# Batch 0 of a Fourier mixing and GELU kernel: part of the second inverse table on VectorE, its copies in another order, fewer spare matmuls at the last table

## The chip, the cores and the metric

One Trainium2 chip, one core of it. The metric is the device time of one execution in microseconds (us), as the median of several runs. Each profile is of one execution, and its own "span" is about 1.8 us shorter than the time measured for that execution.

## The reference

A filter in the frequency domain along the sequence, then a two-layer feed-forward block with exact GELU:

```python
# x: (8, 3008, 256); filt_r, filt_i: (1505, 256); w_in: (256, 2048); w_out: (2048, 256)
X = np.fft.rfft(x, axis=1)
Y = X * (filt_r + 1j * filt_i)[None]
y = np.fft.irfft(Y, n=x.shape[1], axis=1).astype(np.float32).reshape(-1, 256)
h = y @ w_in
g = 0.5 * h * (1.0 + erf(h / sqrt(2)))
return (g @ w_out).astype(np.float32)          # (24064, 256)
```

## The kernel before

The kernel transforms batch 0 as fast as it can (the "front", up to about 40 us), then starts a stream of feed-forward matmuls, into which the transforms of batches 1 to 7 are woven. Only the front is touched. In it, PE is TensorE, DVE is VectorE, ACT is ScalarE and POOL is GpSimd.

The inverse transform needs a table `T3` of 24 slices and a second one, `T3i`, with real and imaginary columns swapped and signed. Both are made from `T2` in three thirds of 8 slices. PE transposes a third into one PSUM bank, and somebody copies it out:

```python
def table_3(self, q):                       # PE, 8 transposes
    self.t3 = ps = self.bank("ps_t3", "n", BF16)
    for i in range(8):
        self.nc.tensor.transpose(ps[:, 128 * i:128 * i + 128], self.T2[:, 8 * q + i]..., self.eye)

def table_3_copy(self, q, turn):            # ACT: T3, and with turn also T3i, from PSUM
    v = self.t3.rearrange("p (k n r) -> p k r n", k=8, r=2)
    self._evac(self.T3[:, 8 * q:8 * q + 8], v, "act")
    if turn:
        for r in range(2):
            self._evac(self.T3i[:, 8 * q:8 * q + 8, r, :], v[:, :, 1 - r, :], "act", self.turn[r])

def table_3_turn(self, q):                  # DVE: T3i from T3 in SBUF (line 256)
    k = slice(8 * q, 8 * q + 8)
    for r in range(2):
        self.nc.vector.tensor_scalar(out=self.T3i[:, k, r, :], in0=self.T3[:, k, 1 - r, :],
                                     scalar1=self.turn[r], scalar2=None, op0=ALU.mult)
```

The work of the front per pair of frequencies (`p` from 0 to 11): `c1t` transposes the data and copies it to `b_sb`, `c2` is two matmuls (line 408) and one DVE product with the filter `F` (line 412), `c3` is the inverse by `T3` and `T3i` (line 430, 16 matmuls for two products). `ps` of `c2` has two PSUM banks, so the matmuls of product p wait for product p - 2.

```python
def c1t(self, q, eng):
    ...                                     # 8 transposes, 4 pairs' worth of data
    n = 1024 // len(eng)
    for i, e in enumerate(eng):             # "act": ScalarE, False: VectorE
        self._evac(b[...][:, n * i:n * i + n], ps[:, n * i:n * i + n], e)

def c2(self, p):
    ...                                     # two matmuls into ps
    nc.vector.tensor_tensor(out=w, in0=ps.unsqueeze(1).to_broadcast([128, 2, 512]),
                            in1=self.F[:, :, 2 * p:2 * p + 2, :]..., op=ALU.mult)
```

Half of `F` is loaded, the other half is a copy. POOL makes these copies for all but the first four frequencies, one instruction (line 97) per product from product 2 on. The loads come in three groups of frequencies (0 to 3, 4 to 11, 12 to 23) in POOL's own DMA queue, behind the loads of x:

```python
for k, n in ((0, 4), (4, 8), (12, 12)):
    m.load_filters(k, n)
m.load_w_in()
nc.gpsimd.memset(m.vt[:, :, 96, :], 0.0)
m.dup_filters(nc.gpsimd, 4, 20)             # POOL, products 2 to 11
...                                         # stage 1 (c1), first third of the table
m.table_3(1)
m.dup_filters(nc.vector, 0, 4)              # DVE, products 0 and 1
m.warm_up(1)                                # spare matmul: nobody reads its result
m.c1t(0, (act, False))
m.table_3_copy(1, True)
m.c1t(1, (act,))
m.c2(0)
m.warm_up(1)
m.c2(1)
m.c1t(2, (act,))
m.warm_up(2)
for q in range(1, 7):
    if q < 6:
        m.c2(2 * q)
        if q + 2 < 6:
            m.c1t(q + 2, (act,))
        m.warm_up(2)
        m.c2(2 * q + 1)
    if q == 3:
        m.table_3(2)
        m.table_3_copy(2, True)
    if q < 6:
        m.c3(2 * q - 2)
        m.warm_up(1)
    ...                                     # the last two inverses
```

## Time and profile before

| | before |
|---|---|
| time, first 6 runs | 773.70 us (773.54 to 773.86) |
| time, all 37 runs of this study | 773.58 us (773.26 to 774.27) |
| span of the trace | 771.8 us |
| first feed-forward matmul (line 482) | 39.94 us |
| from there to the end | 731.9 us |

The table is read from the bottom up. What follows 39.94 us is one PE-bound stream whose length no part of the change touches, so the change is worth what it does to 39.94. The engines, the chain and DVE's products are shown in the prediction.

### The profile page before, as it was taken

Reading aid. Unit: us, or ns where it says so; the run is one execution under the profiler, and the core shown is the slowest. Engines: PE = TensorE matmul, PEld = TensorE weight load, DVE = VectorE, ACT = ScalarE, POOL = GpSimd, SP = SyncE. Lnnn points to the kernel's source line nnn. Section 1 sums busy time; section 2 is a strip of 40 time slices with the busy share of each in tenths; the row PEclk is TensorE's granted clock in tenths of the full one; section 3 lists DMA queues with packets and bytes.
Section 4 is the critical chain, followed back from the end, with each engine's and each line's share of the span. In section 5 each row is a group of like instructions: output and inputs, shape, how many; then the busy total and the mean of one; then the engine's idle time right before and its main releaser. Section 6 shows DMA issues by size and latency. Waiting matters only on the chain.

```text
span 771.8 us, 15050 instructions
## 1 busy us (share of the span) xinstructions
PE 763.7 (99%) x6060; PEld 527.3 (68%) x6060; DVE 397.7 (52%) x734; ACT 568.3 (74%) x980; POOL 63.0 (8%) x154
## 2 busy tenths in 40 slices
PE   7999999999999999999999999999999999999998
PEld 4847675676776766667677767666776776766666
DVE  8856755464545645457463664637646366411011
ACT  7879955897568975699656996579865798666663
POOL 7701100010000200011000110001100000000000
DMA  9894745366253661636516464355553422410111
GB/s 151 147 184 111 153 115 128 128 127 147 58 154 94 137 162 40 193 76 122 143 54 181 85 133 123 81 152 97 122 137 82 138 83 69 123 42 28 42 42 55
DMA packets 87270, 85.66 MB, mean 111 GB/s; under 512 B 6688, under 2 KB 77472, under 8 KB 87200
## 3 DMA queue, kind: packets, MB, share of 16 engines
q1 hardware_dynamic: 78816, 68.70, 31.4%
q0 software_dynamic: 8384, 16.00, 14.8%
q8 instruction: 47, 0.77, 0.4%
q14 instruction: 23, 0.19, 0.1%
HBM read 54.00 MB, written 46.66 MB: 130 GB/s over the span
## 4 chain that ended last, share of the span: by engine, by line
PE 97%; DMA 1%; DVE 1%; POOL 0%; ACT 0%; issue 0%; POOLq 0%; DVEq 0%; SPq 0%
PE ps_o L509 42%; PE ps_h L482 42%; PE ps_s L369 2%; PE ps_s L344 2%; PE ps_s L319 2%; PE ps_s L296 2%; DMA x_sb<-in_x_dram 1%; PE ps_c L430 1%; PE ps_c3t L445 0%; DMA d_sb<-R 0%; PE ps_warm L263 0%; POOL x_sb L83 0%; PE ps_c L408 0%; PE ps_c L459 0%; PE ps_c1t L395 0%; PE ps_e L499 0%
## 5 line engine op out<-in xcount | busy, mean ns | idle before, releaser
L485 ACT ACTIVATE g_sb<-ps_h 128x512 bf16<-128x512 f32 x752 | 438.0, 597 | 183.4 <-PE ps_h L482 172.6
L509 PE MATMUL ps_o<-w_out_sb,g_sb 128*128 128x256 bf16 x2992 | 447.6, 273 | 0.0
L482 PE MATMUL ps_h<-y_sb,w_in_sb 128*128 128x512 bf16 (+3 forms) x1600 | 445.8, 366 | 0.7 <-DVE y_sb L273 0.7
L509 PEld LDWEIGHTS <-g_sb 128*128 128x128 bf16 x2992 | 283.8, 98 | 134.3 <-issue 9.9
L482 PEld LDWEIGHTS <-w_in_sb 128*128 128x128 bf16 x1600 | 154.7, 98 | 23.7 <-issue 1.9
L515 DVE COPY ost<-ps_o 128x512 f32<-128x512 f32 x93 | 63.8, 686 | 143.5 <-PE ps_o L509 143.5
L327 DVE TENSOR_TENSOR p<-ps_s,F 128x512 bf16<-128x512 f32 x84 | 58.1, 691 | 105.9 <-ACT p L326 89.4
L273 DVE TENSOR_SCALAR y_sb<-ps_s 128x376 bf16<-128x376 f32 x112 | 60.9, 548 | 80.8 <-PE ps_s L369 80.8
L271 DVE CAST a_sb<-ps_s 128x512 bf16<-128x512 f32 x112 | 69.3, 682 | 27.7 <-PE ps_s L296 27.7
L271 DVE CAST v_sb<-ps_s 128x512 bf16<-128x512 f32 x84 | 57.4, 684 | 3.0 <-PE ps_s L344 3.0
L325 ACT ACTIVATE p<-ps_s 64x512 bf16<-64x512 f32 x84 | 49.8, 593 | 2.0
L326 ACT CAST p<-ps_s 64x512 bf16<-64x512 f32 x84 | 48.5, 577 | 1.0
L369 PEld LDWEIGHTS <-d_sb 96*128 96x128 bf16 x448 | 30.8, 97 | 25.6 <-DMA d_sb<-R 0.6
L102 POOL COPY gate<-p 1x1 bf16<-1x1 bf16 x48 | 8.5, 176 | 471.5 <-DVE p L329 471.5
L329 DVE TENSOR_TENSOR p<-p 128x512 bf16<-128x512 bf16 x84 | 35.7, 425 | 2.9
L369 PE MATMUL ps_s<-T,d_sb 96*128 96x94 bf16 x448 | 36.3, 204 | 0.1
L328 DVE TENSOR_TENSOR p<-p,F 128x512 bf16<-128x512 bf16 x84 | 34.9, 415 | 0.0
L83 POOL DMA_DIRECT2D x_sb<-in_x_dram x64 | 32.6, 511 | 13.3 <-issue 12.8
L344 PE MATMUL ps_s<-p,T 128*128 128x256 bf16 x168 | 32.1, 273 | 0.0
L319 PE MATMUL ps_s<-b_sb,T 128*128 128x256 bf16 x168 | 32.1, 273 | 0.0
L344 PEld LDWEIGHTS <-T 128*128 128x128 bf16 x168 | 16.4, 98 | 20.0 <-DVE p L329 0.5
L319 PEld LDWEIGHTS <-T 128*128 128x128 bf16 x168 | 16.4, 98 | 13.4
(113 smaller groups left out, 196.6 us busy)
## 6 DMA issues: line engine op xcount, KB each, us to landing
out_dram<-ost SPq DMA_DIRECT2D x93, 256.0 KB, 2.4
x_sb<-in_x_dram POOLq DMA_DIRECT2D x64, 188.0 KB, 3.8
R<-a_sb SPq DMA_DIRECT2D x112, 96.0 KB, 2.1
b_sb<-R SPq DMA_DIRECT2D x28, 384.0 KB, 4.2
R<-v_sb SPq DMA_DIRECT2D x42, 256.0 KB, 3.5
d_sb<-R SPq DMA_DIRECT2D x56, 192.0 KB, 4.8
w_in_sb<-in_moe_w_in_dram POOLq DMA_DIRECT2D x2, 512.0 KB, 9.3
w_out_sb<-in_moe_w_out_dram POOLq DMA_DIRECT2D x2, 512.0 KB, 11.3
```

The lines of the kernel that those rows point to most:

```text
L271: self.nc.vector.tensor_copy(out=out, in_=in_)
L273: self.nc.vector.tensor_scalar(out=out, in0=in_, scalar1=scale, scalar2=None, op0=ALU.mult)
L319: nc.tensor.matmul(ps[:, 256 * i:256 * i + 256], lhsT=self.T2[:, k].rearrange("p a b -> p (a b)"), rhs=self.st[b, "b", k // 6][:, k % 6, : ...
L325: nc.scalar.activation(out=p2[0:64], in_=ps[64:128], func=AF.Copy, scale=-1.0)
L326: nc.scalar.copy(out=p2[64:128], in_=ps[0:64])
L327: nc.vector.tensor_tensor(out=p1, in0=ps, in1=f(0), op=ALU.mult)
L344: nc.tensor.matmul(ps[:, 256 * i:256 * i + 256], lhsT=self.T3[:, k].rearrange("p a b -> p (a b)"), rhs=w[:, 256 * i:256 * i + 256], start= ...
L369: nc.tensor.matmul(ps[:, 94 * i:94 * i + 94], lhsT=d[:, (grp % 2) * 4 + i, 128 * half:128 * half + 128], rhs=t4, start=True, stop=True)
L482: nc.tensor.matmul(ps[:, o:o + n], lhsT=self.w_in_sb[:, dc, jc * 128:jc * 128 + 128], rhs=self.ring[:, dc, off:off + n], start=(dc == 0), ...
L485: nc.scalar.activation(out=self.st["g", t][:, jc, :], in_=ps, func=AF.Gelu)
L509: nc.tensor.matmul(ps[:, tile_i % 2, :], lhsT=g[:, jc, tile_i * 128:tile_i * 128 + 128], rhs=self.w_out_sb[:, jc, :], start=(jc == 0), sto ...
L515: nc.vector.tensor_copy(out=ost, in_=ps)
```

## The change

Its intent: ACT's three copies of the second third stand ahead of the second data block, and DVE waits for that block. So two of the copies go to DVE, into its wait. And the last third stands ahead of 16 matmuls and eats, with spare matmuls, the time in which PE should prepare product 8.

```diff
     m.table_3(1)
+    m.table_3_copy(1, False)
     m.dup_filters(nc.vector, 0, 4)
     m.warm_up(1)
-    m.c1t(0, (act, False))
-    m.table_3_copy(1, True)
+    m.c1t(0, (False, False))
     m.c1t(1, (act,))
     m.c2(0)
+    m.table_3_turn(1)
     m.warm_up(1)
     m.c2(1)
     m.c1t(2, (act,))
@@
             if q + 2 < 6:
                 m.c1t(q + 2, (act,))
-            m.warm_up(2)
+            if q != 3:
+                m.warm_up(2)
             m.c2(2 * q + 1)
-        if q == 3:
-            m.table_3(2)
-            m.table_3_copy(2, True)
         if q < 6:
             m.c3(2 * q - 2)
-            m.warm_up(1)
+            if q == 3:
+                m.table_3(2)
+                m.table_3_copy(2, True)
+            else:
+                m.warm_up(1)
         else:
             m.c3(10, 1)
             m.warm_up(1)
```

## The prediction

> **What bounds the kernel now.** I read the page first, then the critical chain, then the timelines of TensorE (PE), VectorE (DVE), ScalarE (ACT) and GpSimd (POOL) in the first 42 us, then the waits. From the page:
>
> ```profile
> span 771.8 us, 15050 instructions
> PE 763.7 (99%) x6060; PEld 527.3 (68%) x6060; DVE 397.7 (52%) x734; ACT 568.3 (74%) x980; POOL 63.0 (8%) x154
> PE 97%; DMA 1%; DVE 1%; POOL 0%; ACT 0%; issue 0%; POOLq 0%; DVEq 0%; SPq 0%
> ```
>
> PE is busy throughout and is 97% of the chain that ended last. The first feed-forward matmul of line 482 starts at 39.94 us; after it the waits of PE show nothing but small ones, so the remaining 732 us are a stream that only shifts as a whole. The change edits code that runs before that, in batch 0's transform. The question is therefore how much earlier (or later) 39.94 becomes. The loads that the stream needs (x of batch 1, w_in, w_out) are issued by POOL, whose order doesn't change: the eight x loads are issued from 28.57 to 32.1 us and land at most 8.6 us later; the first two are needed at 40.46, the last two at 48.06. A start one microsecond earlier doesn't run into them.
>
> Next, the chain of waits inside that front, from 14 us on:
>
> ```profile
> 14.76 0.60 ACT b_sb L269
> 15.35 0.92 ACT T L269
> 16.27 1.15 ACT T3i L269 x2
> 17.42 0.92 ACT b_sb L269
> 18.39 0.38 PE ps_c L408 x2
> ...
> 23.61 0.45 PE ps_c1t L395 x8
> 24.06 0.43 PE ps_warm L263 x2
> 24.71 0.45 PE ps_t L241 x8
> 25.16 0.89 PE ps_c L430 x16
> ```
>
> First ACT sets the pace (a table copied three ways before it gets to the second transposed block), then PE, back to back, with spare matmuls (ps_warm) and the last table's transposes (ps_t) in the row. DVE's products (line 412) show what that costs:
>
> ```profile
> 15.82 2.36 DVE L412 TENSOR_TENSOR p<-ps_c,F 128x1024 bf16<-128x1024 f32 x2
> 18.86 7.20 DVE L412 TENSOR_TENSOR p<-ps_c,F 128x1024 bf16<-128x1024 f32 x6 [0.68 <-PE ps_c L408]
> 26.58 3.49 DVE L412 TENSOR_TENSOR p<-ps_c,F 128x1024 bf16<-128x1024 f32 x3 [0.52 <-issue]
> 29.98 1.28 DVE L417 TENSOR_TENSOR p<-ps_c,F 128x512 bf16<-128x512 f32 x2
> ```
>
> Twelve products, 1.22 us each. Undisturbed their starts are 1.14 apart (15.82, 16.96; and 26.58, 27.72). The row of six takes 7.20, where five steps of 1.14 and one of 1.22 would be 6.92: products 4 and 6 start 1.28 and 1.29 after their predecessors, each 0.48 after its own matmul began on PE (20.81, 23.23), so they wait for PE. Product 8 starts 1.74 after product 7 (24.84), again 0.48 after its matmul (26.10), which stands behind the transposes, 16 matmuls of the inverse and a spare. So DVE is the engine closest to the bound, PE holds it up in four places, and the front ends with product 11.
>
> **What the Trainium skill says.** "VectorE: DVE Perf Modes", section "The TRN2 errata", gives (N+151)/0.96 ns for an fp32 tensor_tensor; for 1024 elements that is 1224 ns; the trace has 1219. So the product can't be made shorter here, only started sooner. "ScalarE: Activation LUTs", section "What ACT_TABLE_LOAD costs", gives 186 ns + 0.833 ns per element, some 93 ns for a pointer operand and an overlap of some 93 ns: 1039 ns for 1024 elements (the trace has 1023), 706 for 512 with a pointer scale (686 and 694). "SBUF — State Buffer", section "Who interferes with whom": a tensor_scalar in a 2-port mode and a GpSimd instruction lock each other out. The same instruction pair for the first table took 0.34 and 0.35 us at 12.51; POOL then only issued DMAs. The pair that is added falls at 17.0 to 17.5 and POOL's filter copies begin at 17.67, so I expect no collision. "TensorE: Matmul & The Clock Gate", Part 1, says that an idle window of about 3.4 us halves the clock; the granted clock here is 1.00 in every slice, although PE idled 1.27 us before 18.39.
>
> **The change, part by part.**
>
> (1) Second table (the middle third). ACT now only copies T3 from PSUM, 1.02 us, and does it first; the two T3i copies (1.15 us in the chain) go to DVE as line 256. ACT: the last at_sb copy ends at 13.90, T3 is copied until about 14.9, the second b_sb copy (its transposes end near 15.17) runs to about 16.2 instead of 18.31. Off the path: 2.1 us of ACT, of which little can be used, see (3).
>
> (2) The first b_sb block goes wholly to DVE. Before: ACT half 14.76 to 15.36, then the DVE half 15.38 to 15.80 (it waited 0.45 for ACT). After: DVE is free of the filter copies at 14.93, two halves of 0.42: 15.35 and 15.75. The first matmul of line 408 started at 15.40 and can start at about 15.38. Net 0.0; product 0 stays at 15.8.
>
> (3) On DVE the turn comes after product 0: 16.96 plus 2 x 0.26 (the starts of the old pair, 12.51, 12.77, and the next one at 13.03) = 17.48. Product 1 goes from 16.96 to 17.48, product 2 could go at 18.62. Before it waited 0.68 us for PE and began at 18.86. But it reads the filter that POOL copies: that copy runs 17.67 to 18.70. So 18.75. Half a microsecond of work went into a wait, and 0.11 is gained.
>
> (4) From here DVE is ahead or behind PE? I walked PE's order, with 0.22 for a line 408 pair or a spare matmul, 0.45 for eight transposes, 0.89 for line 430, and a PSUM bank of line 408 freed when the product two before it ends. c2(2) at 17.05 (its b_sb is there at 16.2, its bank when product 0 ends); c2(3) at 18.74; line 430 to 19.85; c2(4) 20.07, ready 20.55, product 4's turn is at 21.03. c2(6) 22.49, ready 22.97, turn 23.31. PE no longer holds up products 4 and 6: they save 0.14 and 0.15.
>
> (5) Last table. Three spare matmuls are gone from this group (3 x 0.22 = 0.65 of PE) and the transposes (0.45) go behind the 16 matmuls. c2(7) waits for its bank, 23.43; line 430 from 23.65 to 24.54; transposes to 24.98; c2(8) there, ready at 25.46; product 8's turn is 18.75 + 6 x 1.14 = 25.59. So the 0.60 before product 8 (1.74 - 1.14) goes too, with a margin of only 0.13.
>
> (6) ACT with the last table later: line 430's results copied to 25.6, T3 to 26.54, the two T3i to 27.7; the matmuls of line 430 that need this table start at about 28.2 (bank and products). Slack 0.45. After product 8 DVE ran at its own pace before too, so nothing more is won there.
>
> Sum: 0.11 + 0.14 + 0.15 + 0.60 = 1.00, or from the two starts of product 8, 26.58 - 25.59 = 0.99. Products 9 to 11, the last copy (31.75), the transposes back (32.23) and the first line 482 matmul (39.94) all move by that: to 38.95. 773.69 - 0.99 = 772.70. I put 772.8, since each of the four terms can only fall short.
>
> **Rivals.**
>
> A: *POOL or its filter load becomes the bound.* Product 2 is at 18.75 only because POOL begins at 17.67, when the load lands (the waits have 0.8 us of POOL on that DMA). For it: the margin is zero, and the loads crowd the queues at that time (DMA share above 1.1). Against: later copies run at 1.0 each, faster than 1.14. If the load lands 0.3 later, everything does: about 773.0.
>
> B: *The turn on DVE costs its full 0.52 and PE stays the bound.* For it: DVE is the fullest engine of that stretch (3.86 of 4 us from 20 to 24). It would leave 0.99 - 0.5, about 773.2. Against: the wait of 0.68 is there to be filled.
>
> C: *ACT's last table comes too late for line 430.* Slack 0.45; if ACT is behind by 0.7, the end comes 0.25 later: 772.95.
>
> D: *The clock falls* with fewer spare matmuls. At half speed for one window of 3.4 us, PE's work there would take up to 3.4 us longer, against some 1 us of slack: about 775. Against: the clock stood at 1.00 over a longer idle stretch, and 22 of the 25 spares of that region stay. I give it 3%.
>
> E: *Nothing changes*, as the start of the stream hangs on a DMA that I overlooked: 773.7. The chain before 39.94 shows only PE, DVE and ACT, so 5%.
>
> **Range and chances.** The three runs before lie within 0.32 us of each other, so noise of the median is 0.1 to 0.2. Full gain 772.7; A, B or C in part 773.0 to 773.2; a little better than worked out (product 0 earlier, a load landing sooner) 772.4. So 772.3 to 773.4. Two per cent is 15 us; nothing here is of that size in either direction: chances 0.003, 0.994 and 0.003.
>
> **What would show it.** Right: line 256 with four instructions, the new two near 17.0 and 17.2; product 2 within 0.1 of 18.75; products 2 to 10 in one unbroken row of 1.14 steps with no wait before product 8 (near 25.6); the first line 482 matmul near 38.95, later stages unchanged in length. Step (3) is wrong if product 2 starts past 18.9, step (5) if there is a gap before product 8, step (6) if PE waits for ACT T3i near 28. The prediction as a whole is wrong if the first line 482 matmul moves by less than 0.4 or more than 1.4 us, or if the time after it changes length.

## The result and the profile after

773.17 us as the median of 6 runs, 772.45 to 774.18, against 773.70 (773.54 to 773.86) for the kernel before in the same rounds. The ratio is 0.9994 with a 95% interval of 0.9981 to 1.0007. A ratio is the mean time of one kernel's runs over that of the other's of the same rounds, so not quite the ratio of the medians. By 2% this is "the same", and the range stated holds the median. The interval holds 1, so these six runs alone do not show a gain. What I had not foreseen is the spread: 1.7 us, where the kernel before keeps within 0.3 in the same rounds (and within 1.0 in all its 37 runs).

The first trace after happens to be of the fastest of the six runs (772.45). From its page, the span, and the shares of the chain that ended last:

```profile
span 770.6 us, 15044 instructions
...
PE 94%; DMA 3%; POOL 2%; issue 0%; DVE 0%; POOLq 0%; SPq 0%
```

The span is 1.2 us shorter. The chain now shows DMA and POOL, and this has to be read with care: just ahead of the first line 482 matmul the last of two releasers is a load of x that landed at 38.63, while DVE's last y_sb ended at 38.61. The chain follows the later one. PE waited 0.73 us before that matmul in both kernels, so nothing changed in that wait but its name.

DVE's timeline after (start, duration, instruction, count, and in brackets the idle time before it):

```profile
14.92 0.76 DVE L271 COPY b_sb<-ps_c1t 128x512 bf16<-128x512 bf16 x2
15.82 1.23 DVE L412 TENSOR_TENSOR p<-ps_c,F 128x1024 bf16<-128x1024 f32 x1
16.96 0.35 DVE L256 TENSOR_SCALAR T3i<-T,turn_r 128x512 bf16<-128x512 bf16 x1
17.22 0.35 DVE L256 TENSOR_SCALAR T3i<-T,turn_i 128x512 bf16<-128x512 bf16 x1
17.48 11.40 DVE L412 TENSOR_TENSOR p<-ps_c,F 128x1024 bf16<-128x1024 f32 x10
28.80 1.28 DVE L417 TENSOR_TENSOR p<-ps_c,F 128x512 bf16<-128x512 f32 x2
```

Three rows with two waits have become one row of ten products without a wait; 11.40 is nine steps of 1.13 and one of 1.22. PE's timeline shows why, around product 8 (its line 408 matmuls) and at the start of the stream. Before:

```profile
26.10 0.38 PE L408 MATMUL ps_c<-b_sb,T 128*128 128x256 bf16 x2
...
39.94 0.59 PE L482 MATMUL ps_h<-y_sb,w_in_sb 128*128 128x512 bf16 x2 [0.73 <-DVE y_sb L273]
```

After:

```profile
24.39 0.61 PE L241 MATMUL ps_t<-eye,T 128*128 128x128 bf16 x8
24.83 0.38 PE L408 MATMUL ps_c<-b_sb,T 128*128 128x256 bf16 x2
...
38.76 0.59 PE L482 MATMUL ps_h<-y_sb,w_in_sb 128*128 128x512 bf16 x2 [0.73 <-DMA x_sb<-in_x_dram]
```

The matmuls for product 8 start 1.27 us earlier, directly behind the last table's transposes, and are ready before DVE gets there (25.40). The stream starts 1.18 us earlier and lasts 770.6 - 38.76 = 731.8 us, where it was 731.9.

So this execution shows a gain of 1.2 us. The spans of the other five are 771.7, 772.4, 771.1, 771.1 and 772.0, so two gain 0.7 and three nothing that counts, or lose. Where does the gain go in those? POOL's timeline gives a first hint. Its ten filter copies, in the trace before and in this one:

```profile
17.67 9.98 POOL L97 COPY F<-F 64x1024 bf16<-64x1024 bf16 x10 [0.77 <-DMA F<-in_filt_i_dram]
...
17.41 9.90 POOL L97 COPY F<-F 64x1024 bf16<-64x1024 bf16 x10 [0.55 <-DMA F<-in_filt_i_dram]
```

They start when a filter load lands, 0.26 us earlier than in the trace before, and while the second of the added T3i instructions runs (17.22 to 17.57). Product 2 begins at 18.61, 0.15 behind the end of the first copy (18.46). That is where my rival A had its zero margin.

### The profile page after: what moved, and what is told of

It reads as the page before. It is cut to its first block, busy times and chain, and to the rows that moved or that the text cites. A ratio compares the mean times of both kernels' runs of the same rounds, so it can differ in the third digit from the quotient of the medians.

```text
span 770.6 us, 15044 instructions
## 1 busy us (share of the span) xinstructions
PE 763.5 (99%) x6057; PEld 527.5 (68%) x6057; DVE 398.5 (52%) x737; ACT 566.7 (74%) x977; POOL 62.5 (8%) x154
## 4 chain that ended last, share of the span: by engine, by line
PE 94%; DMA 3%; POOL 2%; issue 0%; DVE 0%; POOLq 0%; SPq 0%
PE ps_o L509 43%; PE ps_h L482 42%; PE ps_s L369 2%; PE ps_s L344 2%; PE ps_s L319 2%; PE ps_s L296 2%; DMA x_sb<-in_x_dram 2%; POOL x_sb L83 1%; DMA F<-in_filt_i_dram 1%; POOL F L97 1%; DMA d_sb<-R 0%; POOL F L92 0%; PE ps_e L499 0%; POOL T1s L282 0%; DVE ost L522 0%
```

## The experiments

Twelve runs, in three calls; the kernels of a call ran on one chip beside the kernel before (773.50, 773.60 and 773.62 in the three). Four theories for the spread: S1 or D, the TensorE clock falls in some runs for want of spare matmuls; F (at first S2), the landing of the filter loads is now on the path; S3, something ahead of the change; and L, which came up with the first slow trace, the two T3i instructions on DVE and POOL's filter copies lock each other out.

### The changed kernel again

No edit.

> The changed kernel unaltered, for the spread of its runs (772.45 to 774.18 before this, where the kernel before kept within 0.32) and a second trace. If the spread is real, the runs again cover over 1 us and this trace need not be the fastest. If the gain of the front is real, a trace shows products 2 to 10 in one row and the first line 482 matmul about 1.2 earlier than 39.94 whenever the filter loads land as in the first trace. Theory S1 (a dropped TensorE clock in some runs, spare matmuls too few): a slow trace shows matmuls at double length inside 14 to 32 us. Theory S2 (the filter load's landing is now on the path): a slow trace shows POOL's filter copies beginning later and DVE products waiting for POOL. Theory S3 (something ahead of 14 us): a slow trace is late before the change begins.

Measured: 772.56 us (772.25 to 773.78), before 773.50 (773.26 to 773.81); ratio 0.9987, interval 0.9973 to 1.0001. The trace is of the slowest of the five, 773.78, with a span of 772.0 and the first line 482 matmul at 40.05. From DVE's timeline:

```profile
17.11 0.34 DVE L256 TENSOR_SCALAR T3i<-T,turn_r 128x512 bf16<-128x512 bf16 x1
17.37 1.13 DVE L256 TENSOR_SCALAR T3i<-T,turn_i 128x512 bf16<-128x512 bf16 x1
18.42 5.73 DVE L412 TENSOR_TENSOR p<-ps_c,F 128x1024 bf16<-128x1024 f32 x5
24.43 5.75 DVE L412 TENSOR_TENSOR p<-ps_c,F 128x1024 bf16<-128x1024 f32 x5 [0.28 <-POOL F L97]
```

and from POOL's:

```profile
17.18 4.17 POOL L97 COPY F<-F 64x1024 bf16<-64x1024 bf16 x4 [0.17 <-POOL vt_sb L577]
23.37 5.95 POOL L97 COPY F<-F 64x1024 bf16<-64x1024 bf16 x6 [2.01 <-DMA F<-in_filt_i_dram]
```

Two losses. First, the second T3i instruction lasts 1.13 in place of 0.35. POOL's first copy began at 17.18, ahead of it, and the T3i instruction ended 0.15 after that copy did (18.35, a copy that took 1.17 instead of 1.03). Note that no idle time is shown: DVE looks busy. Product 1 comes 2.45 after product 0, where it was 1.66 in the fast trace: 0.79 lost. Second, the filters of frequencies 12 to 23 landed at 23.22; POOL waited 2.01 and copied from 23.37 on, its copy for product 6 ended at 24.40, and product 6 began at 24.43. From product 1 to product 6 it took 6.01 instead of 5.66: 0.35 lost. Together with 0.15 that this execution was late ahead of the change (product 0 at 15.97, not 15.82) that makes 1.29, which is 40.05 - 38.76. S1 shows nothing: line 408 pairs still take 0.38 and the granted clock is 1.00. S3 is the 0.15 here; it is larger in a later trace.

### Each part alone

Only the second table's part:

```diff
     m.table_3(1)
+    m.table_3_copy(1, False)
...
-    m.c1t(0, (act, False))
-    m.table_3_copy(1, True)
+    m.c1t(0, (False, False))
     m.c1t(1, (act,))
     m.c2(0)
+    m.table_3_turn(1)
```

> Only the second table's part: T3i on DVE after product 0, first b_sb block on DVE, T3 copy first on ACT; the last table as in the kernel before. My walk: product 2 near 18.65, products 4 and 6 unheld, the third spare-laden group ready for product 8 at 25.84: gain at product 8 about 0.74 (before 26.58), a gap of about 0.35 left before product 8. Median about 773.0. S1: spread as small as before's (all 25 spares stay); S2: spread as large as the changed kernel's.

Only the last table's part: the second half of the change's diff, nothing of the first.

> Only the last table's part: transposes behind line 430's matmuls, three spares fewer, ACT's last table later; the second table as before. My walk: product 2 at 18.86 as before, product 8 at 25.98, gain 0.60 at product 8, median about 773.1. S1: spread large, as three spares are gone; S2: spread small, because product 2 waits for PE at 18.86 anyway and later products run behind POOL.

Measured: the second table alone 772.86 us (772.59 to 773.98), ratio 0.9993 (0.9981 to 1.0006); the last table alone 773.06 (772.79 to 773.36), ratio 0.9994 (0.9981 to 1.0006). DVE's timeline with the second table alone:

```profile
17.42 8.07 DVE L412 TENSOR_TENSOR p<-ps_c,F 128x1024 bf16<-128x1024 f32 x7
25.79 3.49 DVE L412 TENSOR_TENSOR p<-ps_c,F 128x1024 bf16<-128x1024 f32 x3 [0.29 <-issue]
```

and with the last table alone:

```profile
18.78 10.60 DVE L412 TENSOR_TENSOR p<-ps_c,F 128x1024 bf16<-128x1024 f32 x9 [0.69 <-issue]
```

The first keeps the wait before product 8, shortened from 0.52 to 0.29; product 8 is 0.79 earlier than before. The second keeps the wait before product 2 (0.69), and its row of nine holds 0.30 of waits for PE before products 4 and 6, as before, but none before product 8; the stream starts at 39.24, 0.70 earlier. Product 0 was earlier by 0.06 and 0.09 in these two traces, which no part of the change did; without that the gains are 0.73 (0.74 expected) and 0.61 (0.60 expected). So the two gains overlap: 0.73 + 0.61 is more than the 1.18 of both, because each of them makes room on PE ahead of product 8. As for the spread, the kernel with T3i on DVE has the wide one (1.4 us), the kernel with the spares removed the narrow one (0.6). With five runs of each this speaks against S1 and for L or F, but shows neither.

### The spare matmuls put back

```diff
-            if q != 3:
-                m.warm_up(2)
+            m.warm_up(2)
...
             if q == 3:
                 m.table_3(2)
                 m.table_3_copy(2, True)
-            else:
-                m.warm_up(1)
+            m.warm_up(1)
```

> The changed kernel with the three spare matmuls put back (two ahead of product 7's matmul, one behind the last table's transposes). My walk: 0.65 of PE comes back, of which 0.35 shows as a gap before product 8 at 25.84; so about 0.3 to 0.4 slower than the changed kernel's fast runs, median about 773.0. S1: spread of before's size; S2: spread of the changed kernel's size.

Measured: 773.33 us (773.03 to 776.06), ratio 1.0004 (0.9991 to 1.0016). The trace (span 771.5) started 0.56 late ahead of the change, so I count from product 0 to the first line 482 matmul: 23.38 us, against 22.94 for the changed kernel's fast trace and 24.12 before. So the three spares cost 0.44 (0.3 to 0.4 expected).

The 0.56 is theory S3, and PE's timeline shows what it is. Line 385, far ahead of the change, transforms batch 0's x; its last row of 16 matmuls, first in the trace before and then in this one:

```profile
10.59 0.84 PE L385 MATMUL ps_c<-T1c,x_sb 94*128 94x96 bf16 x16
...
11.16 0.84 PE L385 MATMUL ps_c<-T1c,x_sb 94*128 94x96 bf16 x16 [0.64 <-DMA x_sb<-in_x_dram]
```

A load of x landed 0.58 later than in the trace before (at 11.03, not 10.45, by the chain of waits), and product 0 came 0.56 later. The row began at 10.05 to 11.16 over the 14 traces. So this is a source of spread of its own, which no part of the change touches.

The four other runs lie within 0.65 us, which would suit S1; but one run took 776.06 with a granted clock of 0.998, so on the spread this experiment settles nothing. The reading of 0.998 says little: the clock was 1.00 up to 765 us in every trace here, and lower, if at all, only at the very end (0.83 from 765 us on in a trace of a fast run, 772.22, with 0.999). There is no trace of the run of 776.06, so what it was stays open. It is in any case the one kernel here that has all 25 spares and the added DVE work.

### The two T3i instructions earlier and later

Earlier, behind the b_sb copies and ahead of product 0:

```diff
     m.c1t(0, (False, False))
+    m.table_3_turn(1)
     m.c1t(1, (act,))
     m.c2(0)
-    m.table_3_turn(1)
```

> The changed kernel, with the two T3i instructions of the second table before product 0 (right behind the b_sb copies) in place of behind it. They then run near 15.7 to 16.2, well before POOL's first filter copy (16.9 to 17.8 in the six traces so far), so they can't meet it. Theory L (the lock between these two and POOL's copy makes the slow runs): both take 0.35 in every trace, product 1 starts near 17.35 to 17.5, and runs near 773.8 vanish: all between 772.1 and 772.9. Theory F (only the second filter load's landing makes them): the spread stays over 1 us.

Later, behind product 1:

```diff
     m.c2(0)
-    m.table_3_turn(1)
     m.warm_up(1)
     m.c2(1)
+    m.table_3_turn(1)
```

> The same two instructions behind product 1, that is near 18.1, where POOL surely copies. Theory L: at least one of the two lasts 0.6 to 1.3 instead of 0.35, product 2 starts 0.3 to 1.2 later than the 18.61 of the changed kernel's first trace (unless it waits for POOL anyway), the median is 0.3 to 1.2 above the changed kernel's fast runs: 772.7 to 773.6, in most runs. Theory F: both last 0.35, and the median is the changed kernel's, as the sum of DVE's work ahead of product 2 is the same.

Measured: early 772.36 us (772.31 to 773.08, one run above the 772.9 expected), before 773.60 (773.28 to 774.27), ratio 0.9985 (0.9973 to 0.9998); late 773.25 (773.03 to 773.80), ratio 0.9997 (0.9984 to 1.0009). DVE's timeline, late:

```profile
15.78 2.36 DVE L412 TENSOR_TENSOR p<-ps_c,F 128x1024 bf16<-128x1024 f32 x2
18.05 0.35 DVE L256 TENSOR_SCALAR T3i<-T,turn_r 128x512 bf16<-128x512 bf16 x1
18.31 1.13 DVE L256 TENSOR_SCALAR T3i<-T,turn_i 128x512 bf16<-128x512 bf16 x1
19.37 10.26 DVE L412 TENSOR_TENSOR p<-ps_c,F 128x1024 bf16<-128x1024 f32 x9
```

and POOL's second copy in it:

```profile
18.14 1.16 POOL L97 COPY F<-F 64x1024 bf16<-64x1024 bf16 x1
```

The 1.13 is back, to the hundredth, in the place where POOL surely copies. The second T3i instruction ended at 19.44, 0.14 after that copy (19.30). The copy for product 2 was done at 18.18, so product 2 did not wait for data: it waited for the instruction ahead of it. Product 2 comes 3.59 after product 0 here, 2.79 in the changed kernel's fast trace, with the same DVE work between. The stream starts at 39.50, not 38.76: those 0.80 less 0.06 that DVE caught up at product 0 and later. Early:

```profile
15.75 0.34 DVE L256 TENSOR_SCALAR T3i<-T,turn_r 128x512 bf16<-128x512 bf16 x1
16.01 0.42 DVE L256 TENSOR_SCALAR T3i<-T,turn_i 128x512 bf16<-128x512 bf16 x1
16.35 12.52 DVE L412 TENSOR_TENSOR p<-ps_c,F 128x1024 bf16<-128x1024 f32 x11
```

POOL's first copy began at 17.18 in this trace too, as in the slow trace above, and cost nothing. In the code only the place of the two instructions differs. With the same lengthening in two traces, each time to 0.14 or 0.15 past the end of POOL's copy, L is shown. The other order cost DVE nothing: in the trace with the spares put back POOL's first copy began at 17.82, 0.04 after the second T3i instruction (0.35), and it was the copy that took longer, 1.20 in place of 1.03.

### w_in later, to free the filter loads

```diff
-    m.load_w_in()
-
     nc.gpsimd.memset(m.vt[:, :, 96, :], 0.0)
-    m.dup_filters(nc.gpsimd, 4, 20)
+    m.dup_filters(nc.gpsimd, 4, 14)
+    m.load_w_in()
+    m.dup_filters(nc.gpsimd, 18, 6)
```

> The changed kernel, with the two w_in loads (512 KB each) issued behind seven of POOL's filter copies in place of ahead of them; w_in then lands near 34, before 38.8 where it is needed. Theory F with w_in as its cause: the second filter load lands by about 21, product 6 never waits for POOL, and the spread halves. If the filter load's landing depends on other loads only, it stays between 21.2 and 23.4. Theory L: the spread stays, since the first load still lands near 17, now perhaps earlier, so that POOL starts into the two T3i instructions more often: median up to 0.5 slower than the changed kernel's.

The same with the early T3i:

> Both edits together. Theories L and F both true: no run above 772.6, median 772.1 to 772.4, spread of 0.4. If only L is true: as the first kernel of this call.

Measured: 772.96 us (772.80 to 774.28), ratio 0.9994 (0.9981 to 1.0008), and 772.86 (771.95 to 772.96), ratio 0.9987 (0.9975 to 1.0000). The first kept its spread (1.5 us), as expected of theory L, but its trace shows no lock (the T3i instructions took 0.34 and 0.35). The second has four of five runs above the 772.6 expected, and a spread of 1.0 us. From DVE's timeline of the first:

```profile
17.44 9.27 DVE L412 TENSOR_TENSOR p<-ps_c,F 128x1024 bf16<-128x1024 f32 x8
26.88 2.36 DVE L412 TENSOR_TENSOR p<-ps_c,F 128x1024 bf16<-128x1024 f32 x2 [0.17 <-POOL F L97]
```

The edit made its own wait: issuing w_in takes POOL 1.1 us, and the copy for product 9 came too late (0.17 here, 0.46 in the other). I had thought that POOL was ahead by enough. As to the question, whether w_in holds up the second filter load: it landed at 21.61 and 21.64, not by 21. In the eight traces with w_in in its old place in which the chain of waits runs over this load, it landed between 21.18 and 23.22. From its issue to its landing it took 7.04 and 7.03 with w_in later, and 6.20 to 8.08 in those eight. That speaks against w_in, though two traces do not settle it. The same chains show a part of the answer: POOL waited for loads of batch 0's x before it issued the filter loads, and the last one was issued at 14.57 to 15.49. The larger part, 6.20 or 8.08 for the same load, stays open.

### All three on one chip, and T3i on ACT

The changed kernel, the kernel with the early T3i, and the kernel before, without further edits:

> The changed kernel once more, beside the next two on the same chip. Theory L and F: median between 772.3 and 773.2, some runs above 773.4; if its trace is a slow one, it shows a T3i instruction of over 0.5 us near 17.3, or product 6 waiting for POOL, or both.

> The kernel with the two T3i instructions ahead of product 0 once more, for a comparison on one chip: median 772.2 to 772.6, no run above 773.2, so 0.2 to 0.6 below the changed kernel's median.

> The kernel before, for a second trace: product 2 again near 18.86 and held by PE, not by POOL (whose first copy ends 17.9 to 18.8), products 4 and 6 again 1.28 behind their predecessors; 773.2 to 774.3, as its 24 runs so far.

And a kernel in which DVE gets nothing extra: ACT makes T3i from PSUM as before the change, but one copy behind `c1t(1)` and one behind `c1t(2)`, where it waits anyway:

```diff
     m.c1t(1, (act,))
+    m.table_3_turn_act(1, 0)     # one of the two ACT copies of table_3_copy
     m.c2(0)
-    m.table_3_turn(1)
     m.warm_up(1)
     m.c2(1)
     m.c1t(2, (act,))
+    m.table_3_turn_act(1, 1)
```

> The changed kernel, but both T3i instructions of the second table stay on ACT (straight from PSUM as before the change), placed into ACT's waits: one behind the second b_sb copy, one behind the third (each waits 0.56 and 0.26 there, and one costs 0.57). DVE goes from product 0 straight to product 1 at 16.96 and could start product 2 at 18.10. If DVE's 0.52 us bounds that stretch, product 2 comes 0.3 to 0.5 earlier than in the kernel with the early turn (18.6) and the median is 771.9 to 772.2. If POOL's first filter copy bounds it (ends 17.9 to 18.8), product 2 starts right behind that copy, the gain is 0 to 0.3, and product 6 meets the second load more often, so the spread grows.

Measured, beside 773.62 us (773.34 to 774.17) for the kernel before:

| kernel | us, median (range) | ratio (95%) |
|---|---|---|
| changed | 772.64 (772.22 to 773.20) | 0.9987 (0.9975 to 1.0000) |
| early T3i on DVE | 772.96 (771.96 to 773.10) | 0.9987 (0.9973 to 1.0000) |
| T3i on ACT | 772.96 (772.23 to 773.42) | 0.9990 (0.9977 to 1.0002) |
| before, as a fourth | 773.40 (773.27 to 773.47) | 0.9996 (0.9983 to 1.0010) |

The early T3i was not the faster one this time, against my expectation. Its trace is of its slowest run (773.10): the first filter load landed late, POOL's first copy began at 18.29 and ended at 19.32, and product 2 began at 19.36, after a wait of 0.38. That is theory F at the first load. The changed kernel's trace is of its fastest run (no run above 773.4 came up, against the expectation); POOL began at 17.56, clear of the T3i instructions (0.35 each).

With T3i on ACT the DVE row had no gap at product 2, but at product 6. DVE's timeline:

```profile
16.33 6.88 DVE L417 TENSOR_TENSOR p<-ps_c,F 128x1024 bf16<-128x1024 f32 x6
23.96 5.75 DVE L417 TENSOR_TENSOR p<-ps_c,F 128x1024 bf16<-128x1024 f32 x5 [0.75 <-POOL F L97]
```

and POOL's:

```profile
17.43 3.98 POOL L97 COPY F<-F 64x1024 bf16<-64x1024 bf16 x4
22.89 5.95 POOL L97 COPY F<-F 64x1024 bf16<-64x1024 bf16 x6 [1.47 <-DMA F<-in_filt_i_dram]
```

This trace was 0.51 late at product 0 (theory S3). From there product 2 came after 2.27, not 2.79: the 0.5 us taken off DVE was gained, and then came back as a wait of 0.75 for the second filter load (landed at 22.74, copied by 23.92). In this execution the filters' arrival is the next limit. Over five runs, taking this work off DVE showed no gain in time; what it would be worth when the load lands early was not traced. The kernel before is not as exposed, and its second trace shows the reason:

```profile
18.75 7.21 DVE L412 TENSOR_TENSOR p<-ps_c,F 128x1024 bf16<-128x1024 f32 x6 [0.68 <-PE ps_c L408]
```

POOL's first copy began at 17.12 there, 0.01 after the second of two T3i instructions behind product 0 would have begun, and the second load's first copy began at 21.92. Product 2 still waited for PE, and product 6 came at 23.59, 0.6 after its filters were copied (22.95). Its waits for PE hide whatever the loads do, up to that margin.

Nine of the fourteen traces, with the start of each step in us. The last column is the first line 482 matmul (line 487 in the kernel with T3i on ACT, which has five lines more):

| trace (time of that run) | POOL copy 1 | product 0 | product 1 | product 2 | product 6 | product 8 | stream |
|---|---|---|---|---|---|---|---|
| before (773.62) | 17.67 | 15.82 | 16.96 | 18.86 | 23.71 | 26.58 | 39.94 |
| before, second trace (773.41) | 17.12 | 15.71 | 16.85 | 18.75 | 23.59 | 26.47 | 39.83 |
| changed (772.45) | 17.41 | 15.82 | 17.48 | 18.61 | 23.14 | 25.40 | 38.76 |
| changed, slow run (773.78) | 17.18 | 15.97 | 18.42 | 19.55 | 24.43 | 26.71 | 40.05 |
| changed, third trace (772.22) | 17.56 | 15.88 | 17.54 | 18.67 | 23.20 | 25.46 | 38.82 |
| early T3i (772.33) | 17.18 | 16.35 | 17.48 | 18.61 | 23.13 | 25.40 | 38.74 |
| early T3i, slow run (773.10) | 18.29 | 16.64 | 17.77 | 19.36 | 23.89 | 26.15 | 39.50 |
| late T3i (773.11) | 17.15 | 15.78 | 16.92 | 19.37 | 23.89 | 26.15 | 39.50 |
| T3i on ACT (773.26) | 17.43 | 16.33 | 17.47 | 18.60 | 23.96 | 26.23 | 39.58 |

The changed kernel has 16 runs with a mean of 772.94 and a median of 772.86 us (772.22 to 774.18), five of them from 773.20 up. The kernel with the early T3i has 10 runs, mean 772.63, median 772.56, none above 773.10. The kernel before has 37, mean 773.59. So the change is worth about 0.65 us on average (four times the standard error of the 16 runs' mean, 0.15, though in each of its three comparisons the interval reaches 1), and the early T3i about 0.3 more. The second figure mixes calls, and in the one call with both kernels their ratios were the same to four digits, so I call it likely, not shown; that the early place removes the lock is shown by the traces.

## Why the prediction was right or wrong

**The time and the class.** 772.8 was predicted, 773.17 measured in the first six runs and 772.86 in all 16; the range of 772.3 to 773.4 holds both medians. Right, but in part by luck. The sum of 0.99 was worked out for an execution without a disturbance, and such a one gained 1.18 (the fast trace); 0.14 of the difference is a filter load that happened to land earlier. The medians of the six runs are only 0.53 apart. That the two nearly cancel was not foreseen: losses that vary from run to run were a rival, not a term of the sum.

**Step 1, ACT.** T3's copy ended at 14.83 (about 14.9 predicted), the second b_sb copy at 16.14 (16.2). Right.

**Step 2, b_sb on DVE.** No gain, product 0 at 15.82 as before. Right.

**Step 3, the turn.** 16.96, 17.22 and product 1 at 17.48, to the hundredth, in the fast trace. Product 2 at 18.61, not 18.75, since the filters landed 0.26 earlier than in the trace I worked from. But the sentence "so I expect no collision" failed: it rested on one trace, in which POOL began at 17.67. Over 14 traces of all kernels POOL's first copy begins between 16.95 and 18.29, and in five of them ahead of 17.22; only one of these five had its T3i instructions behind product 0, and there it collided. The collision cost 0.79. The skill's section that I named states the mechanism, and I had the number to apply it with, but took a single observation of a DMA's landing for a fixed time. This is the step that was wrong. In the one slow run of the changed kernel that has a trace it is 0.79 of the 1.29 lost; the slow runs without a trace can't be assigned.

**Step 4, products 4 and 6.** They save 0.15 and 0.17 (2.42 to 2.27 and 2.43 to 2.26 from the product two before). 0.14 and 0.15 predicted. Right.

**Step 5, product 8.** 2.87 from product 6 became 2.26, a gain of 0.61; 0.60 predicted. Its matmuls began at 24.83, 24.98 predicted. Right. The sum of the four in the fast trace is 0.25 + 0.15 + 0.17 + 0.61 = 1.18, which is what the stream moved. The parts alone (0.73 and 0.61, counted from product 0) show that both are needed for it, and the spares put back cost 0.44.

**Step 6, ACT's last table.** The T3i copies ended at 27.51, and the line 430 matmuls that need them began at 28.02: slack 0.51, 0.45 predicted. Rival C did not happen.

**The rivals.** A happened, in a wider form than I gave it: at the first load (wait 0.38 in one trace of the early T3i), and at the second load, which I had dismissed ("later copies run at 1.0 each, faster than 1.14"). That argument looked at POOL's pace and forgot that the fifth copy waits for another load. B did not happen: PE held up no product in the fast trace, and the turn cost less than the wait it filled (product 2 came 2.79 after product 0, where it was 3.04). D left no mark: the granted clock was 1.00 in the front of every trace; one run without a trace (776.06) stays unexplained. Its size was also worked out wrongly: a window of 3.4 us at half speed loses 1.7 us of work, not 3.4. E is refuted as it was put: in all 14 traces 731.6 to 732.2 us follow the first matmul of the stream, wherever that lies. But its sentence that the chain ahead of 39.94 shows only PE, DVE and ACT holds from 14 us on only; followed further back, the chain of the trace before hangs on a load of batch 0's x, from 4.79 to 10.45, and that is the load which came late in theory S3.

What stays open: why the same load lands up to 1 us (x) or 2 us (filters) apart in different executions, and the cause of each slow run that has no trace.

## What to carry to other kernels

When a wait on a steady engine is filled with work, the next limit may be one that varies from run to run, such as a load's landing; then the median gains less than one good trace shows, and several traces, above all one of a slow run, tell more than a close reading of the best one. Before placing a VectorE instruction on 16-bit data in SBUF, ask what GpSimd may be doing at that time in any execution, not only in the one traced; here a place some tenths of a microsecond earlier cost nothing (38.74 and 38.76 at the start of the stream). The instruction that was locked out showed as a long one, not as idle time, so compare durations of the same instruction between traces.

## What the Trainium skill lacked or had wrong

- "SBUF — State Buffer", section "Who interferes with whom": its rule that the one who comes first keeps the shared ports for its whole instruction agrees with the traces. It says that the loser measures slower, but not how that looks in a profile: no idle time, but a duration of 1.13 us in place of 0.35 on DVE, and 1.16 to 1.20 in place of 1.03 on POOL for a copy that came just after a T3i instruction.
- "DMA: Bandwidth & Descriptors", section "Anatomy of one DMA — SWDGE (gpsimd) path": its fit of 2.0 us plus size over 436 GB/s gives 2.5 us for one 192 KB load. In the busy queue of this front the loads of filt_i of that size took 6.2 to 7.9 us (median of two loads, in three traces), and the page gives no spread between executions of one program; the last of these loads landed between 21.18 and 23.22.
- "VectorE: DVE Perf Modes", section "The TRN2 errata": its row for SBUF to SBUF, 58 + FD/4 cycles at 0.96 GHz, would be an estimated 0.19 us for the 512 bf16 elements of one T3i instruction, if it runs at four elements a cycle, which no run here shows; it took 0.34 to 0.35, with the next one starting 0.26 after it. The page says itself that the row is short for single operations, by about 92 cycles; with these the estimate is 0.29. The measured value here comes with a per-partition pointer scalar, for which the page has no term.
